# A planned mLSTM + MLP kernel: one pool for the 4 KB tiles, paired Softplus, merged attention products, another planned order

## The chip, the core and the metric

The kernel runs on one core of a Trainium2 chip. The metric is the device time in microseconds (us) of one execution, the median over runs. One more execution was recorded by the hardware profiler; all rows of the trace come from that one.

## The reference, cut to what matters

Four sequences (B) with eight heads (H), 768 steps (S) and head size 40 (D) go through a gated linear attention with a running maximum, and its output, 320 wide, goes token by token through an MLP with Softplus and Erf:

```python
for t in range(S):
    m_new = np.maximum(f_gate[:, :, t] + m, i_gate[:, :, t])
    f_stab = np.exp(f_gate[:, :, t] + m - m_new)
    i_stab = np.exp(i_gate[:, :, t] - m_new)
    C = f_stab * C + i_stab * outer(v_t, k_t);  n = f_stab * n + i_stab * k_t
    y[:, :, t] = sigmoid(o_gate_t) * (C @ q_t) / max(abs(n . q_t), 1)
h = x @ w_in                          # (3072, 320) @ (320, 2048)
g = h * erf(softplus(h))
out = g @ w_out                       # (2048, 320)
```

(shortened; `x` is `y` with the heads side by side). The MLP's weights arrive as 64-bit floats, and all is computed to float32 accuracy.

## The kernel before, in words

**Attention.** Time is cut into six chunks of 128 steps. A chunk of one sequence is an attention step s (24 of them; 0 to 3 are the first chunk). For each chunk a gate part (lines 257 to 322) scans the running maximum, sums the log gates (`scan`, `g`, `sum`, lines 268 to 291) and cuts them into three bf16 pieces (`split`); from the second chunk on twelve small DMAs (`rhs`, line 319) put rows of it into `rhsE`. An attention step (lines 324 to 518) then has these runs on TensorE, each named by its lines:

- pe (367, 369): the exponents of all heads, two PSUM banks, then Exp on ScalarE (375) and the causal mask on POOL (380);
- S (397): the scores, two banks, multiplied into the masked weights on VectorE (412);
- pq (422): the decay of each row, multiplied into q on VectorE (430); only from the second chunk on;
- ph (439, 443): the numerators and denominators from the state and from the chunk itself; pk (455): what the chunk adds to the state, from `vg` (406);
- tr (500): transposes of the step's output (480 to 494), whose high part goes to `xh` (ScalarE, 513) and low part to `xl` (VectorE, 517).

All of these use four PSUM banks, the tag `pa`.

**Weights.** Each of 22 tiles of 512 KB raw weights (12 of `w_in`, 10 of `w_out`) is loaded on SP's queue and decoded from 64-bit words (lines 523 to 548): a first step on ScalarE (530), two bit steps on VectorE (535, 536), a rounded high part on ScalarE (541, tiles `wh`, `woh`) and the low part on POOL (547, `wl`, `wol`). A decode holds one of two work tiles (`bits`) from 530 to 547. The raw tile itself takes a free place among the MLP's own tiles hb, e, gh and gl, of which a few must stay free (`KEEP`).

**MLP.** A block k is 256 tokens, two attention steps. A phase f is half a block's hidden layer (24 phases, the first four in the order (0,0), (1,0), (0,1), (1,1)). A phase has two groups g of 512 hidden units: two up runs of 16 matmuls into the two banks `h` (630), each copied to `hb` (on ScalarE, 639, in the first two phases, then on VectorE, 641), Softplus (648) and Erf (652) on ScalarE, the product with h (VectorE, 656), its rounded part gh (ScalarE, 661) and the rest gl (VectorE, 666), and two down runs of 12 matmuls (691, 692, 694) that add to the banks `po0` and `po1`. High and low parts make each product exact enough: three matmuls in place of one. Exp, Softplus and Erf need three different function tables, and a load of a table (ACT_TABLE_LOAD) stands before each change.

**What sets the order.** Nothing is ordered by hand. `Plan.issue` (lines 77 to 166) holds every part with its engine, cost, table, buffers and targets, lets a list scheduler run in model time, and emits the parts in order of their start; each engine then works in this order, waiting on semaphores. A chain (lines 734 to 748) fixes the order of the table users: both Softplus and then both Erf of a phase, then the Exp of the step that belongs to it (`AHEAD`). `SLOTS` gives the number of buffers of each tag, `FIRST`, `PHASE` and `BEHIND` the targets.

Of the kernel before, what the change touches and what calls it, by code (L numbers as in the profile page):

```python
# [18 lines left out]
L = 128  # L19
# [21 lines left out]
class Buf:  # L41
    def __init__(self, tag=None, keep=None):
        self.tag, self.keep, self.users, self.left = tag, keep, [], 0
# [6 lines left out]
class Plan:  # L50
# [26 lines left out]
    def issue(self):  # L77
# [3 lines left out]
        for p in parts:  # L81
            for x in p.after:
                x.succ.append((p, True))
            for x in p.order:
                x.succ.append((p, False))
            p.wait = len(p.after) + len(p.order)
        topo, left = [p for p in parts if not p.wait], {p.n: p.wait for p in parts}
# [11 lines left out]
        for p in parts:  # L99
            for b in p.held:  # L100
                b.left += 1
        slots = {tag: [0.0] * n for tag, n in self.slots.items()}
# [5 lines left out]
        def can(p):  # L108
            t = max(free[p.engine], p.ready)
            for b in p.new:  # L110
                if b.keep:
                    at = [(min(slots[tag]), i, tag) for i, (tag, n) in enumerate(b.keep.items()) if len(slots[tag]) > n]
                    if not at:
                        return None
                    t, b.tag = max(t, min(at)[0]), min(at)[2]
                    continue
                s = slots[b.tag]
                need = sum(x.tag == b.tag for x in p.new)
                if len(s) < need:
                    return None  # L120
                t = max(t, sorted(s)[need - 1])
            return t + self.TABLE * (p.table is not None and len(p.table) > 1 and table not in p.table)

        while len(out) < len(parts):
# [27 lines left out]
            for b in p.new:  # L152
                slots[b.tag].remove(min(slots[b.tag]))
            for b in p.held:
                b.left -= 1
                if not b.left:
                    slots[b.tag].append(max(u.done for u in b.users if hasattr(u, 'done')))
# [7 lines left out]
        out.sort(key=lambda p: (p.start, out.index(p)) if False else p.start)  # L165
# [3 lines left out]
SLOTS = dict(pa=4, h=2, po0=1, po1=1, qk=3, kvo=3, dm=5, vg=4, xh=2, xl=2, o_sb=4, hb=4, e=3, gh=3, gl=3,  # L169
             bits=2, spl=2, x0=1, gt=1, m_c=2, aL=3, den=2)  # L170
FIRST, PHASE, BEHIND = 20.0, 18.0, 1.3
AHEAD = {s: s - 4 for s in range(B * NC)}
AHEAD.update({0: -1, 1: -1, 2: -1, 3: -1, 4: 2, 5: 2, 6: 3, 7: 3})
KEEP = dict(gl=1, gh=1, e=2, hb=2)
# [4 lines left out]
def tile_mlstm_moe(  # L179
# [23 lines left out]
    def new(pool, shape, dtype, tag):  # L203
        return pool.tile(shape, dtype, name=tag, bufs=SLOTS[tag])

# [51 lines left out]
    def gate_chunk(c):  # L257
# [10 lines left out]
        @make(f'scan{c}', 'DVE', 0.65, after=[load, last.scan if c else p_small], new=[m_c], use=[gt] + ([last.m_buf] if c else []))  # L268
# [8 lines left out]
        @make(f'g{c}', 'DVE', 0.66, after=[scan], new=[x0], use=[gt, m_c])  # L277
        def g():
            v.x0 = new(sb, [128, 3, L], F32, "x0")
            y = v.x0[:, 2]  # L280
            nc.vector.tensor_tensor(y, v.gt[:, 1], v.m[:, 0:L], op=ALU.add)
            nc.vector.tensor_tensor(y, y, v.m[:, 1:L + 1], op=ALU.subtract)
            if c == 0:
                nc.vector.memset(y[:, 0:1], 0.0)

        @make(f'sum{c}', 'DVE', 1.05, after=[g, p_small], use=[gt, m_c, x0])
        def total():
            nc.vector.tensor_tensor_scan(
                out=v.x0[:, 1], data0=v.x0[:, 2], data1=zero.to_broadcast([128, L]), initial=0.0, op0=ALU.add, op1=ALU.add)
            nc.vector.tensor_tensor(v.x0[:, 0], v.gt[:, 0], v.m[:, 1:L + 1], op=ALU.subtract)  # L290
            nc.vector.tensor_tensor(v.x0[:, 0], v.x0[:, 0], v.x0[:, 1], op=ALU.subtract)
# [10 lines left out]
        @make(f'split{c}', 'DVE', 2.6 if c else 1.9, after=[v.exp or total, p_cst], new=[spl], use=[x0])  # L302
# [21 lines left out]
    def attention(s):  # L324
# [16 lines left out]
        def load():  # L341
            t = new(sb, [128, 2, NPR, L], F32, "qk")
# [3 lines left out]
        @make(f'loadv{s}', 'SP', 0.45, kb=484.0, new=[kvb])  # L346
        def loadv():
            n = new(sb, [128, KVO + 64], F32, "kvo")
            nc.sync.dma_start(n[:, 0:KVO], kvo[c, b])
            v.kn = n[:, 0:DM].rearrange("p (h d) -> p h d", d=D)  # L350
            v.v1 = n[:, DM:KV].rearrange("p (h d) -> p h d", d=V1)
            v.th = n[:, KV:KVO]
            v.y = n[:, KV:KVO + 64]

        @make(f'rows{s}', 'POOL', 1.2 if c else 0.5, after=[G.split, p_zeros], use=[G.spl_buf],
# [4 lines left out]
        v.pe, ex, sel = [], [], []  # L360
        for j in range(2):
            @make(f'pe{s}', 'PE', 0.24 if c else 0.46, after=[rowsp, *G.rhs, p_rhsE[c % 2]], new=[peb[j]], target=mid(14 - j),
                  order=[step[s - 2].S] if s > 1 else [])
            def pe(j=j):
                spl = splB[b]
# [4 lines left out]
            v.pe.append(pe)  # L370

            @make(f'ex{s}', 'ACT', 0.5, after=[pe], new=[dmb[j]], use=[peb[j]], table=('exp',))
# [5 lines left out]
            @make(f'sel{s}', 'POOL', 0.85, after=[e], use=[dmb[j]])  # L378
# [6 lines left out]
        @make(f'th{s}', 'ACT', 0.38, after=[loadv], use=[kvb], table=('exp', 'er'))  # L385
        def th():
# [3 lines left out]
        @make(f'S{s}', 'PE', 0.95, after=[load, *ex], new=psb, use=[qkb], mode=1, target=mid(11),  # L390
              order=[step[s - 2].ph_] if s > 1 else [])
        def Sp():
# [427 lines left out]
```

## Time and profile before

| | us |
|---|---|
| median of three runs | 512.39 |
| the runs | 512.39, 510.31, 515.2 |
| the profiled execution | 513.25 |
| its span, first to last instruction | 511.2 |

The profile calls the engines PE (TensorE), PEld (its weight loads), DVE (VectorE), ACT (ScalarE), POOL (GpSimd) and SP (which here only issues DMAs). In a row of a chain or timeline stand the start, the duration and what ran; in a group the line, engine, operation, tiles as out<-in and shapes, the count, the busy time with the mean ns of one, and the idle time before them with what ended it. A matmul's own duration overlaps with its neighbours; in the chain each has only what it adds. "issue" as what ended a wait means that the profile shows nothing that was waited for. The matmuls of the float32 attention products count twice in the trace.

### The profile page before, as it was taken

The page shows a single profiled execution, that of the slowest core. Times are in us where ns is not written, and L with a number is a line of the kernel's source. Part 1 is how long each engine was busy: PE and PEld are TensorE (multiplying, and loading weights), DVE is VectorE, ACT ScalarE, POOL GpSimd, SP SyncE. Part 2 cuts the span into 40 slices and gives each one's busy share as a digit, 9 for nine tenths or more (in the row PEclk, how much of TensorE's full clock was granted, in tenths as well). Part 3 has the DMA queues.
Part 4 walks back from the last instruction along what each step waited for, and adds up shares of the span by engine and source line. Part 5 has one row for each costly group of instructions (what it writes and reads, how often), then busy time and mean ns, then how long its engine had stood idle before and what let it go on. Part 6 is the DMA issues. An engine that isn't in the chain of part 4 may idle for free.

```text
span 511.2 us, 13994 instructions
## 1 busy us (share of the span) xinstructions
PE 470.2 (92%) x6120; PEld 448.2 (88%) x6120; DVE 347.6 (68%) x609; ACT 363.7 (71%) x424; POOL 104.3 (20%) x158
## 2 busy tenths in 40 slices
PE   3497678959999999999999999999999999999977
PEld 2376678949999999999999999999999999999977
DVE  3579859897887766787766885765974665555431
ACT  4268897985357977977977877887787795566651
POOL 5173425272220101121101111001211010000000
PEclk9758797978999999999999999999999999999997
DMA  7999623102261220122131131131131100000000
GB/s 193 281 294 264 168 83 125 55 1 73 64 185 40 73 82 29 66 56 78 54 99 35 42 103 36 40 100 36 40 102 36 39 28 2 3 27 0 27 0 27
DMA packets 17765, 39.40 MB, mean 77 GB/s; under 512 B 2920, under 2 KB 9064, under 8 KB 17704
## 3 DMA queue, kind: packets, MB, share of 16 engines
q1 hardware_dynamic: 17704, 38.51, 26.3%
q8 instruction: 48, 0.79, 0.6%
q14 instruction: 13, 0.11, 0.1%
HBM read 34.45 MB, written 3.93 MB: 75 GB/s over the span
## 4 chain that ended last, share of the span: by engine, by line
PE 78%; DMA 6%; DVE 5%; issue 4%; ACT 4%; POOL 1%; SPq 1%; DVEq 0%; POOLq 0%; ACTq 0%
PE h L630 31%; PE po L691 11%; PE po L692 10%; PE po L694 10%; PE pa L397 4%; DMA kvo<-in_kvo_dram 3%; PE pa L439 3%; PE pa L443 2%; DMA gl<-in_w_in_dram 2%; PE pa L367 2%; PE pa L500 2%; DVE hb L656 1%; PE pa L422 1%; PE pa L455 1%; DVE bits L536 1%
## 5 line engine op out<-in xcount | busy, mean ns | idle before, releaser
L630 PE MATMUL h<-xh,wh 128*128 128x256 f32 x576 | 163.9, 292 | 5.2 <-ACT wh L541 3.4
L630 PE MATMUL h<-xl,wh 128*128 128x256 f32 x576 | 161.7, 288 | 1.2 <-DVE xl L517 0.9
L691 PE MATMUL po<-woh,gh 128*128 128x320 f32 x384 | 124.2, 334 | 3.1 <-ACT gh L661 3.1
L630 PEld LDWEIGHTS h<-xh,wh 128*128 128x128 f32 x576 | 112.4, 195 | 6.7 <-ACT wh L541 3.6
L692 PE MATMUL po<-wol,gh 128*128 128x320 f32 x384 | 116.4, 314 | 0.0
L630 PEld LDWEIGHTS h<-xl,wh 128*128 128x128 f32 x576 | 112.6, 195 | 1.8 <-DVE xl L517 1.2
L630 PE MATMUL h<-xh,wl 128*128 128x256 f32 x384 | 110.8, 289 | 1.4 <-POOL wl L547 1.4
L641 DVE COPY hb<-h 128x512 f32<-128x512 f32 x88 | 60.3, 688 | 67.0 <-PE h L630 66.6
L648 ACT ACT_TABLE_LOAD x40 | 51.3, 1283 | 46.6 <-DVE hb L641 46.2
L656 DVE TENSOR_TENSOR hb<-e,hb 128x1024 f32<-128x1024 f32 x48 | 60.0, 1265 | 32.2 <-ACT e L652 32.1
L691 PEld LDWEIGHTS po<-woh,gh 128*128 128x128 f32 x384 | 73.8, 192 | 6.1 <-ACT gh L661 3.4
L648 ACT ACTIVATE e<-hb 128x1024 f32<-128x1024 f32 x48 | 50.7, 1059 | 39.0 <-DVE hb L641 32.8
L630 PEld LDWEIGHTS h<-xh,wl 128*128 128x128 f32 x384 | 74.8, 195 | 1.7 <-POOL wl L547 1.7
L692 PEld LDWEIGHTS po<-wol,gh 128*128 128x128 f32 x384 | 74.1, 193 | 0.3
L694 PE MATMUL po<-woh,gl 128*128 128x320 f32 x384 | 72.8, 312 | 0.1
L380 POOL TENSOR_SCALAR_AFFINE_SELECT dm<-dm 128x512 f32<-128x512 f32 x48 | 32.6, 698 | 152.0 <-ACT dm L375 151.7
L666 DVE TENSOR_TENSOR gl<-hb,gh 128x1024 fp32r<-128x1024 f32 x48 | 59.5, 1241 | 3.0 <-PE po L694 2.2
L694 PEld LDWEIGHTS po<-woh,gl 128*128 128x128 f32 x384 | 61.2, 191 | 0.4 <-DVE gl L666 0.4
L661 ACT ACTIVATE gh<-hb 128x1024 fp32r<-128x1024 f32 x48 | 50.6, 1057 | 8.3 <-DVE hb L656 7.9
L488 POOL TENSOR_TENSOR kvo<-kvo,den 128x320 f32<-128x320 f32 x24 | 20.1, 836 | 149.7 <-DVE kvo L484 111.1
L652 ACT ACTIVATE e<-e 128x1024 f32<-128x1024 f32 x48 | 48.4, 1051 | 0.3
L412 DVE TENSOR_TENSOR dm<-pa,dm 128x512 f32<-128x512 f32 x48 | 32.0, 684 | 13.2 <-PE pa L397 13.2
(81 smaller groups left out, 614.6 us busy)
## 6 DMA issues: line engine op xcount, KB each, us to landing
kvo<-in_kvo_dram SPq DMA_DIRECT2D x24, 484.0 KB
qk<-in_qk_dram SPq DMA_DIRECT2D x24, 416.0 KB
out_dram<-o_sb SPq DMA_DIRECT2D x24, 160.0 KB
gh<-in_w_in_dram SPq DMA_DIRECT2D x3, 512.0 KB
gl<-in_w_in_dram SPq DMA_DIRECT2D x4, 256.0 KB
gl<-in_w_in_dram SPq DMA_DIRECT2D x2, 512.0 KB
e<-in_w_in_dram SPq DMA_DIRECT2D x2, 512.0 KB
hb<-in_w_out_dram SPq DMA_DIRECT2D x3, 320.0 KB
```

Of the source, the lines that this page charges most:

```text
L380: nc.gpsimd.affine_select(out=v.w[j], in_=v.w[j], pattern=[[0, NPR], [1, L]], compare_op=ALU.is_ge, fill=0.0, base=0, channel_multiplier=-1)
L412: nc.vector.tensor_tensor(v.w[j], v.ps[j], v.w[j], op=ALU.mult)
L630: nc.tensor.matmul(V.h[i][:, n % 2 * T:(n % 2 + 1) * T], w, m, start=(q == 0), stop=(q == len(ops) - 1))
L641: nc.vector.tensor_copy(V.hb[:, i * 512:(i + 1) * 512], V.h[i])
L648: nc.scalar.activation(V.e, V.hb, AF.Softplus)
L652: nc.scalar.activation(V.e, V.e, AF.Erf)
L656: nc.vector.tensor_tensor(V.hb, V.e, V.hb, op=ALU.mult)
L661: nc.scalar.activation(V.gh, V.hb, AF.Copy)
L666: nc.vector.tensor_tensor(V.gl, V.hb, V.gh.bitcast(F32), op=ALU.subtract)
L691: nc.tensor.matmul(K.po[b], V.gh[:, ts], woh[:, w], start=start, stop=False)
L692: nc.tensor.matmul(K.po[b], V.gh[:, ts], wol[:, w], start=False, stop=False)
L694: nc.tensor.matmul(K.po[b], V.gl[:, ts], woh[:, w], start=False, stop=stop)
```

## The change

- **One pool.** The tags qk, kvo, hb, e, gh and gl (3 + 3 + 4 + 3 + 3 + 3 places) become one tag `big` with 19 places of 4 KB. Raw weights are tiles of it too; `CAPS` limits each kind in the planner (raw: 10), and `KEEP` holds back places. To fit into 4 KB, K, V and the output gate of a step come by two DMAs, and y lies over the gate and k.
- **Paired Softplus.** For the phases in `BURST` (0, 2, 4, 6 to 20) the first Softplus also waits for the copies of the second group.
- **Merged runs.** The two halves of pe are one part, pq is at the head of S, pk at the tail of ph, and steps follow each other more strictly (S of a step after ph of the step before).
- **Moved work.** The gate steps `g` and the new `rest` go from VectorE to POOL; `vg` of steps 1, 2, 3, 5 and 7 too; copies of h for phases 0 to 4 and 6 (not 0 and 1) are on ScalarE; six low parts (`LO_DVE`) go from POOL to VectorE; the state copy of step 1 goes to ScalarE.
- **The order.** Costs in the planner are altered, the penalty for a change of table is doubled, and `NUDGE`, a table of some 190 numbers, shifts the due times of single parts.

```diff
-SLOTS = dict(pa=4, h=2, po0=1, po1=1, qk=3, kvo=3, dm=5, vg=4, xh=2, xl=2, o_sb=4, hb=4, e=3, gh=3, gl=3,
+SLOTS = dict(pa=4, h=2, po0=1, po1=1, big=19, dm=5, vg=4, xh=2, xl=2, o_sb=4,
              bits=2, spl=2, x0=1, gt=1, m_c=2, aL=3, den=2)
...
+CAPS = dict(qk=4, kvo=4, hb=4, e=3, gh=3, gl=3, raw=10)
...
+KEEP = {'raw': 4, 'qk': 1, 'kvo': 1}
+HB_ACT = {0, 1, 2, 3, 4, 6}
+BURST = {0, 2, 4, 6, 7, 8, 9, 10, 11, 12, 13, 14, 15, 16, 17, 18, 19, 20}
+LO_DVE = {'i01', 'i30', 'i31', 'o0', 'o2', 'o6'}
+GATE = {1: 0, 2: 3, 3: 7, 4: 11, 5: 15}
+VG_POOL = {1, 2, 3, 5, 7}
+SK_ACT = {1}
+NUDGE = {
+    'S0': 15.8, 'S1': 0.2, 'S2': 13.8, 'S4': 4.2, 'S5': -3.1, 'S6': 1.5, 'S7': -7.1, 'deci10': -17.8,
...
+    def big(name, dtype=F32, n=1024):
+        return sb.tile([128, n], dtype, name=name, tag="big", bufs=SLOTS["big"], padded_shape=[128, 1024])
...
-            n = new(sb, [128, KVO + 64], F32, "kvo")
-            nc.sync.dma_start(n[:, 0:KVO], kvo[c, b])
...
+            n = big("kvo")
+            nc.sync.dma_start(n[:, DM:KVO], kvo[c, b][:, 0:KV])
+            nc.sync.dma_start(n[:, 0:DM], kvo[c, b][:, KV:KVO])
...
         def Sp():
+            if c > 0:
+                v.pq_ = t = bank(NPR, L)
+                for p in range(NPR):
+                    nc.tensor.matmul(t[:, p], selP[:, 2 * p:2 * p + 2].rearrange("p a b -> p (a b)"),
+                                     splB[b][:, 1, :], start=True, stop=True)
             v.ps = [bank(NPR, L) for _ in range(2)]
...
+    for f, v in enumerate(phases):
+        if f in BURST:
+            v.sp[0].after.extend(v.copies[2:])
```

The counts of matmuls are the same in both programs; table loads are 100 before and 70 now. Three places of the two orders follow, each before and then now.

ScalarE, from the Softplus of phase 2 to the first Exp of step 4 (e is the tile of Softplus, or of Erf where it is also the input; bits, wh and woh are decode; dm the exponents; hb the copies of h):

```order
L648 ACT_TABLE_LOAD
L648 ACTIVATE e<-hb 128x1024
L541 ACTIVATE woh<-bits 128x512
L530 ACT_TABLE_LOAD
L530 ACTIVATE bits<-gh 128x512
L530 ACTIVATE bits<-e 128x512
L648 ACT_TABLE_LOAD
L648 ACTIVATE e<-hb 128x1024
L652 ACT_TABLE_LOAD
L652 ACTIVATE e<-e 128x1024 x2
L375 ACT_TABLE_LOAD
L375 ACTIVATE dm<-pa 128x512
```

```order
L684 ACTIVATE hb<-h 128x512
L694 ACT_TABLE_LOAD
L694 ACTIVATE e<-hb 128x1024 x2
L698 ACT_TABLE_LOAD
L698 ACTIVATE e<-e 128x1024 x2
L422 ACT_TABLE_LOAD
L422 ACTIVATE dm<-pa 128x512 x2
```

The two Softplus stand in a row behind the last copy, the decode steps are ahead of them, and five table loads became three.

SP's queue, the last loads of the output weights (raw now; gl, hb and e before) and the twelve small rows of the second chunk's gates (rhsE):

```order
L594 DMA gl<-in_w_out_dram 128x256
L594 DMA hb<-in_w_out_dram 128x640
L594 DMA hb<-in_w_out_dram 128x384
L594 DMA e<-in_w_out_dram 128x512 x2
L319 DMA rhsE_69<-spl 1x8x128 x6
L594 DMA hb<-in_w_out_dram 128x384
L594 DMA hb<-in_w_out_dram 128x640
L319 DMA rhsE_69<-spl 1x8x128 x6
```

```order
L620 DMA raw<-in_w_in_dram 64x1024 x2
L363 DMA rhsE_69<-spl 1x8x128 x3
L607 DMA raw<-in_w_in_dram 128x1024 x2
L363 DMA rhsE_69<-spl 1x8x128 x9
L639 DMA raw<-in_w_out_dram 128x384
L639 DMA raw<-in_w_out_dram 128x640
L307 DMA gt<-in_gates_dram 128x2x128
L639 DMA raw<-in_w_out_dram 128x128
```

The gate rows now go ahead of the last five tiles of the output weights, where they stood behind four of them.

TensorE at the end (of every down run only its last row, four matmuls with gl, is shown; gl's number tells the group, po0 and po1 the two halves of the tokens), from the last matmul of the last up run on:

```order
L630 MATMUL h_6559<-xl_5965,wh_79 128x256
L694 MATMUL po0_6531<-woh_81,gl_6527 128x320 x4
L694 MATMUL po1_6546<-woh_81,gl_6527 128x320 x4
L694 MATMUL po0_6531<-woh_81,gl_6609 128x320 x4
L694 MATMUL po1_6546<-woh_81,gl_6609 128x320 x4
L694 MATMUL po0_6531<-woh_81,gl_6613 128x320 x4
L694 MATMUL po1_6546<-woh_81,gl_6613 128x320 x4
```

```order
L675 MATMUL h_6539<-xl_6003,wh_79 128x256
L740 MATMUL po1_6343<-woh_81,gl_6416 128x320 x4
L740 MATMUL po0_6574<-woh_81,gl_6499 128x320 x4
L740 MATMUL po0_6574<-woh_81,gl_6521 128x320 x4
L740 MATMUL po1_6605<-woh_81,gl_6499 128x320 x4
L740 MATMUL po1_6605<-woh_81,gl_6521 128x320 x4
L740 MATMUL po0_6574<-woh_81,gl_6621 128x320 x4
L740 MATMUL po1_6605<-woh_81,gl_6621 128x320 x4
L740 MATMUL po0_6574<-woh_81,gl_6637 128x320 x4
L740 MATMUL po1_6605<-woh_81,gl_6637 128x320 x4
```

The last phase's four down runs are the last four in both; ahead of them stand two before and five now.

More of the change, by code (lines that the diff above doesn't have):

```diff
@@ L275, in gate_chunk @@
         v.scan = scan
-        @make(f'g{c}', 'DVE', 0.66, after=[scan], new=[x0], use=[gt, m_c])
+        @make(f'g{c}', 'POOL', 1.0, after=[scan], new=[x0], use=[gt, m_c])
         def g():
@@ L300, in gate_chunk @@
         n = 3 if c > 0 else 2
[L302 removed]
+        @make(f'split{c}', 'DVE', 3.0 if c else 2.0, after=[v.exp or total, rest, p_cst], new=[spl], use=[x0])
         def split():
@@ L358, in rowsp, with pe @@
             nc.gpsimd.tensor_copy(splB[b][rows], G.spl[rows, 0:(3 if c > 0 else 2):(2 if c > 0 else 1)])
[L360 to L365, printed above, removed]
+        ex, sel = [], []
+        @make(f'pe{s}', 'PE', 0.42 if c else 0.86, after=[rowsp, *G.rhs, p_rhsE[c % 2]], new=peb, target=mid(14), mode=3,
+              order=[step[s - 1].S] if s > 0 else [])
+        def pe():
+            spl = splB[b]
+            for j in range(2):
                 v.pe_[j] = t = bank(NPR, L)
@@ L369, in pe @@
                     nc.tensor.matmul(t[:, p], r[:, 2 * p + j, :], spl[:, 1, :], start=False, stop=(p == NPR - 1))
-            v.pe.append(pe)
-            @make(f'ex{s}', 'ACT', 0.5, after=[pe], new=[dmb[j]], use=[peb[j]], table=('exp',))
+        v.pe = [pe]
+        for j in range(2):
+            @make(f'ex{s}', 'ACT', 0.56, after=[pe], new=[dmb[j]], use=[peb[j]], table=('exp',))
             def e(j=j):
@@ L413, in attention @@
             w.append(wp)
-        v.pq, qa = None, None
+        v.pq, qa = Sp, None
         if c > 0:
-            @make(f'pq{s}', 'PE', 0.26, after=[rowsp, p_selP], new=[pqb], target=mid(9),
-                  order=[step[s - 1].ph_, Sp])
-            def pq():
-                v.pq_ = t = bank(NPR, L)
-                for p in range(NPR):
-                    nc.tensor.matmul(t[:, p], selP[:, 2 * p:2 * p + 2].rearrange("p a b -> p (a b)"),
-                                     splB[b][:, 1, :], start=True, stop=True)
-            v.pq = pq
-            @make(f'qa{s}', 'DVE', 0.83, after=[pq, load], new=[aLb], use=[pqb, qkb], order=[Sp])
+            @make(f'qa{s}', 'DVE', 0.83, after=[Sp, load], new=[aLb], use=[pqb, qkb])
             def qa():
@@ L444, in ph @@
                                          start=(c == 0), stop=(c == 0 or j == 1))
+            if not last:
+                v.pk = bank(NPR, V1)
+            for p in range(0 if last else NPR):
+                for d in (slice(0, 32), slice(32, D)):
+                    for j in range(2):
+                        nc.tensor.matmul(v.pk[64 * j + d.start:64 * j + d.stop, p], v.kn[:, 2 * p + j, d], v.vg[j][:, p],
+                                         start=True, stop=True)
         v.ph_ = ph
@@ L521, in tile_mlstm_moe, with decode @@
     wout = []
-    def decode(name, raw, rawb, ready, hi, lo, engine='POOL'):
+    def decode(name, raw, rawb, ready, hi, lo):
+        engine = 'DVE' if name in LO_DVE else 'POOL'
         v = SimpleNamespace()
         vb = Buf('bits')
-        @make(f'val{name}', 'ACT', 0.58, after=ready, new=[vb], use=[rawb], table=('exp', 'er'))
+        @make(f'val{name}', 'ACT', 0.7, after=ready, new=[vb], use=[rawb], table=('exp', 'er'))
         def val():
```

163 lines of the change are left out of this document (83 added, 80 removed), and 22 rows, old and new, of the table NUDGE.

## The prediction

> **What bounds the kernel now.** I read the page first, then the busy time by stage, the chain that ended last, TensorE's waits, and ScalarE's groups in the stage where TensorE has holes. The page's first line:
>
> ```profile
> PE 470.2 (92%) x6120; PEld 448.2 (88%) x6120; DVE 347.6 (68%) x609; ACT 363.7 (71%) x424; POOL 104.3 (20%) x158
> ```
>
> 92% is an average over stages that have different limits. Busy time by stage, the cuts set where TensorE's behaviour changes:
>
> ```profile
> 0.00:39.90 39.90, 23.16 (x420) 18.71 (x422) 23.09 (x51) 18.69 (x31) 19.25 (x37) 0.79 0.94 260
> 39.90:110.80 70.90, 54.80 (x461) 51.02 (x459) 60.42 (x93) 60.99 (x84) 32.26 (x28) 0.86 0.43 117
> 110.80:115.80 5.00, 3.59 (x130) 3.00 (x130) 4.12 (x8) 4.94 (x6) 1.77 (x2) 0.50 0.01 3
> 115.80:491.30 375.50, 375.22 (x5048) 362.56 (x5045) 254.57 (x455) 271.79 (x298) 50.99 (x92) 1.00 0.18 54
> 491.30:511.20 19.90, 13.42 (x72) 12.89 (x70) 5.43 (x5) 7.33 (x8) 0.00 (x0) 0.81 0.05 17
> ```
>
> After the stretch and its length come busy us of PE, PEld, DVE, ACT, POOL, then granted clock, DMA share, GB/s. From 115.8 to 491.3 TensorE has 0.28 us free at clock 1.00. Nothing can be won there without fewer matmuls, and the matmul counts of the two programs are equal. ScalarE has 104 us free in it. What can be won lies before 115.8 us (first the loads at 0.94 of the DMA engines, then ScalarE at 61.0 of 70.9 us and VectorE at 60.4) and in the last 20 us. The end of the chain:
>
> ```profile
> 467.29 3.83 PE h L630 x32
> ...
> 489.32 1.93 PE h L630 x16
> 491.27 0.70 DVE hb L641
> 492.05 1.06 ACT e L648
> 493.13 1.28 ACT L652
> 494.43 1.07 ACT e L652
> 495.52 1.24 DVE hb L656
> 496.77 1.07 ACT gh L661
> 497.88 0.64 PE po L691
> ...
> 501.45 0.27 PE po L691
> ...
> 504.32 0.15 PE po L691
> ...
> 507.89 0.44 ACT o_sb L712
> ```
>
> and two of TensorE's waits (total, times, longest):
>
> ```profile
> PE pa L443 <- issue: 6.4, 1, 6.4
> ...
> PE po L691 <- ACT gh L661: 3.1, 1, 3.1
> ```
>
> The last up run ends at 491.25. Its results pass copy, Softplus, table load, Erf, product and rounding, and are there at 497.84, 6.6 us later. Only two down runs stand in between, so TensorE is idle for 3.1 us, and the next two runs go at a slow clock: 497.88 to 501.45 is 3.57 us and 501.45 to 504.32 is 2.87 us, where the last two, at the full clock, take 1.78 each (504.32 to 507.89).
>
> **The change part by part.**
>
> *The tail.* In the new order nine down runs, not six, follow the last up run: five instead of two lie ahead of the first that needs its results. Five by 1.78 is 8.9 us against the 6.6 us chain, so the wait goes (3.1 us) and with it the slow clock (3.57 + 2.87 - 2 x 1.78 = 2.9). One output copy now stands between the two Erf on ScalarE (0.44 by L712); it holds only the second half, which is needed two runs later. **-6.0 us**; bounds -3.1 (the clock stays slow) and -6.4.
>
> *The stage where ScalarE and VectorE are the limit.* Eight down runs and sixteen up runs precede the first down run of phase 2 in both programs. Before, it starts at 115.79, after the last weight has been decoded:
>
> ```profile
> 39.93 1.28 ACT L648 ACT_TABLE_LOAD   x1
> ...
> 110.17 0.63 ACT L541 ACTIVATE woh<-bits 128x512 fp32r<-128x512 f32 x1 [0.66 <-DVE bits L536]
> ```
>
> ```profile
> 109.56 3.01 POOL L547 TENSOR_TENSOR wol<-bits,woh 128x512 fp32r<-128x512 f32 x2
> ```
>
> ```profile
> 115.79 0.64 PE L691 MATMUL po<-woh,gh 128*128 128x320 f32 x1
> ```
>
> ScalarE's groups between these two points, 39.9 to 110.8 us:
>
> ```profile
> L648 ACT ACT_TABLE_LOAD x5 | 6.4, 1283 | 0.1
> L648 ACT ACTIVATE e<-hb 128x1024 f32<-128x1024 f32 x6 | 6.3, 1057 | 0.1
> ...
> L541 ACT ACTIVATE woh<-bits 128x512 fp32r<-128x512 f32 x10 | 6.0, 623 | 1.6 <-DVE bits L536 1.6
> ...
> L652 ACT ACT_TABLE_LOAD x3 | 3.8, 1283 | 0.0
> L639 ACT ACTIVATE hb<-h 128x512 f32<-128x512 f32 x6 | 3.6, 592 | 3.2 <-PE h L630 3.2
> L530 ACT ACTIVATE bits<-gl 128x512 f32<-128x512 f32 x5 | 3.4, 673 | 0.7 <-POOL wol L547 0.7
> ...
> L530 ACT ACT_TABLE_LOAD x2 | 2.6, 1283 | 0.0
> ...
> L297 ACT ACT_TABLE_LOAD x1 | 1.3, 1283 | 0.0
> L375 ACT ACT_TABLE_LOAD x1 | 1.3, 1283 | 0.0
> L513 ACT ACTIVATE xh<-pa 128x384 fp32r<-128x384 f32 x2 | 1.0, 481 | 0.0
> ```
>
> That is 12 table loads. Between the same two points the new order has 9. It has one Softplus more, two first decode steps and three high-part copies fewer (they come earlier, when ScalarE is half idle), two transposed copies fewer and four copies of h more (moved from VectorE): -3 x 1.283 + 1.057 - 2 x 0.673 - 3 x 0.623 - 2 x 0.481 + 4 x 0.592 = -4.6 us of work. Of the 9.9 us idle I let half go, 4.9: VectorE, whose decode it waits for, gives copies of h and gate steps away, and loads no longer wait for one of few buffers; bounds 0 and 9.9. The first Softplus I leave at 40: it now waits for all four copies of phase 0, but the input weights are loaded ahead of the later attention tiles. It could start 6.4 us earlier if TensorE's pause of 6.4 us inside an attention product (all its inputs there) does not come back. So the last high part ends at 40 + 70.9 - 4.6 - 4.9 = 101.4, its low part needs 1.5 more on POOL (half of 3.01), and products of step 4 and scores of step 5 go first: I take 4.0 in all, where it took 5.0. First down run of phase 2 at 105.4, **-10.4 us**; bounds -4 and -17. The new order has also done the scores of step 5 by then (1.1 us by L397's row below): **-1.1**. Steps 4 and 5 follow each other closely, and the score run of step 4 has only one exponent run behind it to cover VectorE: **+1.5**; 0 to 5.
>
> By the Trainium skill, ScalarE: Activation LUTs, "What ACT_TABLE_LOAD costs", a switch costs 1.28 us and a drain of 1.38 more; the estimate from that page for three loads is -8.0 in place of -3.8. The trace does not show the drain: above, a Softplus ends at 493.11, the load starts at 493.13 and the Erf at 494.43.
>
> *All the other table loads* (27 of the 30 that go) lie after 115.8, where TensorE hides ScalarE: nothing. What pays for them is that the first Softplus of a phase waits for the fourth copy. Before, one phase in the steady stage reads
>
> ```profile
> 240.22 1.28 ACT L648 ACT_TABLE_LOAD   x1 [3.20 <-DVE hb L641]
> ...
> 250.46 1.09 ACT L375 ACTIVATE dm<-pa 128x512 f32<-128x512 f32 x2
> ```
>
> ```profile
> 252.98 1.16 PE L397 MATMUL pa<-qk 40*128 40x128 f32 x16
> ```
>
> The exponents end at 251.55, the score run that reuses their banks starts at 252.98: 1.4 us of cover. Now one more Softplus (about 1.0) lies in that queue, and the row-decay products (some 0.2 us) go ahead of the scores: 0.7 us of cover are left. I cost it at nothing; if it is gone, see the third rival.
>
> *Merged products:* in the steady stage both orders have the same four attention runs for a step, and over all 292 runs stand for 300. A boundary costs little (two up runs in one piece take 3.83 us, two apart 2 x 1.93): 0, at most -0.3. *The shared pool:* raw tiles get places of their own; its worth is in the idle time above. *K/V/O in two pieces:* 24 more DMA issues on SP's queue at
>
> ```profile
> 43.34 0.33 SPq L349 DMA_DIRECT2D kvo<-in_kvo_dram  x1
> ```
>
> one each: 2.6 us over the eight of the first stage, 0.1 us for each piece of weight behind them; hidden, because those loads are bound by bytes. *Gate steps and some vg on POOL, six low parts on VectorE:* POOL's low part takes 1.30 us for 512 columns; before 115.8 six less are -7.8, and eight vg of 164 and twelve gate steps of 128 columns at that rate +7.2. Nothing, but a collision is dear:
>
> ```profile
> 61.29 2.33 DVE L656 TENSOR_TENSOR hb<-e,hb 128x1024 f32<-128x1024 f32 x1
> ```
>
> ```profile
> 61.23 1.30 POOL L547 TENSOR_TENSOR wol<-bits,woh 128x512 fp32r<-128x512 f32 x1 [3.07 <-ACT woh L541]
> ```
>
> 2.33 beside a POOL instruction, 1.24 alone.
>
> **Sum.** The profiled execution: 513.25, its span 511.2. 511.2 - 6.0 - 10.4 - 1.1 + 1.5 = 495.2, and 2.05 around it give 497.25. The median of the three runs, 512.39, is 0.86 below the profiled time: **496.4 us**.
>
> **The rivals.**
>
> 1. *The first stage tightens fully.* The pause of 6.4 us doesn't return, Softplus starts at 36 and all idle time of ScalarE goes: another -4 and -5.0, 487 us. For it: raw tiles are no longer held back, and DMA is busy for 0.43 of the stretch only. Against: VectorE has 60.4 us of work in the same 70.9, so both queues would have to be nearly gapless.
>
> 2. *Only the tail is won.* The decode stays as slow, because its two work tiles, not ScalarE, set its pace: a decode holds one of them from its first step on ScalarE to its low part on POOL, and there are two in both programs. Then phase 2's first down run stays at 115.8: 496.4 + 10.4 = 507 us. For it: ScalarE waits for decode steps of VectorE (1.6) and for POOL's low parts (0.7) in the groups above. Against: 3.2 of its idle time, the largest piece, belong to copies that wait for TensorE.
>
> 3. *Slower: the exponents come late for the scores.* In the steady stage the last copy of a phase queues behind two VectorE instructions of 1.24 each. Everything on ScalarE shifts by 2.5 us, 1.8 more than its cover, and TensorE waits in each of sixteen steps: +28, 525 us. It decides from 0.7 + 16.0/16 = 1.7 us of delay on (there it eats the gain). For it: the fourth copy was the last of two short queues and is now ahead of all. Against: VectorE is busy for 254.6 of 375.5 us, and 72 copies against 88 remain on it.
>
> That the program doesn't do what it says is no rival: the table loads (100 to 70) and the tail stand in its order.
>
> **How the numbers follow.** Forecast 0.59, first rival 0.17, second 0.15, third 0.09. The forecast's own range, from the bounds of its terms, is 489 to 505. The whole range, **485 to 510**, takes in the first rival but for its far end, and the second; about 0.2 is left out. A measurement of this kernel tells about 1%, 5.1 us, from no change. Faster by more: 0.59 + 0.17 + 0.06 of the second (it lies on the bound) = 0.82. Within 1%: 0.09 of the second and 0.02 of the third, 0.11. Slower: 0.07.
>
> **What would show it.** The tail is right if TensorE has no wait of over 0.3 us after its last up run and clock 1.00 to the end. The first stage is right if the first down run of phase 2 starts at 101 to 110 us and ScalarE's stretch before the last high part has 9 table loads. The cover is right if in the steady stage TensorE waits for no bank of the exponents; a wait there of over 1 us for each step makes the prediction wrong, as does a first down run of phase 2 at 115 or later. Loads at over 250 GB/s past 51 us would say that bytes, not engines, set the first stage.

## The result and the profile after

The changed kernel takes 496.23 us, the median of four runs (496.03 to 496.45); the kernel before, run beside it, 513.37 (510.31 to 515.2). The ratio is 0.967, with a 95% interval of 0.962 to 0.972. The forecast was 496.4. The profiled execution is one of the four: 496.05, its span 494.3. The page's first line, and the busy time by stage with the cuts at the first Softplus table load, the end of the last decoded weight, and the steady stage:

```profile
PE 464.1 (94%) x6120; PEld 442.2 (89%) x6120; DVE 327.4 (66%) x562; ACT 333.6 (67%) x412; POOL 113.4 (23%) x187
```

```profile
0.00:42.40 42.40, 26.98 (x564) 22.26 (x564) 29.24 (x63) 24.30 (x44) 29.70 (x55) 1.00 0.96 261
42.40:103.00 60.60, 49.39 (x446) 45.98 (x446) 45.70 (x66) 56.31 (x78) 25.25 (x27) 0.89 0.55 155
103.00:110.00 7.00, 6.82 (x65) 6.25 (x69) 6.45 (x11) 5.30 (x9) 2.22 (x2) 0.52 0.25 77
110.00:478.00 368.00, 367.91 (x4971) 354.96 (x4963) 241.23 (x421) 242.05 (x278) 56.23 (x104) 1.00 0.17 49
478.00:494.30 16.30, 12.99 (x89) 12.73 (x87) 4.80 (x4) 5.61 (x8) 0.00 (x0) 1.00 0.09 31
```

The second row answers to the stretch of 70.9 us before: it is 60.6 now, with ScalarE busy for 56.31 and VectorE for 45.70 (60.99 and 60.42 before). The fourth shows a TensorE without a hole at clock 1.00, as before. The last has no slow clock any more. The three points on which the forecast hung, from ScalarE's and TensorE's timelines:

```profile
42.38 1.28 ACT L694 ACT_TABLE_LOAD   x1
...
102.39 0.61 ACT L586 ACTIVATE woh<-bits 128x512 fp32r<-128x512 f32 x1
```

```profile
94.15 1.16 PE L449 MATMUL pa<-qk 40*128 40x128 f32 x14 [1.44 <-ACT dm L422]
...
97.60 0.59 PE L413 MATMUL pa<-rhsE,splB 128*128 128x512 bf16 x1 [1.97 <-DVE qk L473]
...
103.18 2.05 PE L449 MATMUL pa<-qk 40*128 40x128 f32 x14 [0.57 <-DVE kvo L528]
105.16 0.63 PE L737 MATMUL po<-woh,gh 128*128 128x320 f32 x1
```

The first Softplus table load comes at 42.38 (39.93 before), the last high part ends at 103.0 (110.80), and the first down run of phase 2 starts at 105.16 (115.79). The chain that ended last, from the last up run on:

```profile
473.23 1.92 PE h L675 x16
475.15 0.15 PE po L737
...
490.41 0.60 PE po L740 x4
491.03 0.44 ACT o_sb L758
```

From 475.15 to 491.01 nine down runs follow without a wait, 1.76 us each.

Three lengths cut each execution at two places that all programs have, the first Softplus table load and the first down run of phase 2: the time to the one, the **stretch** from the one to the other, and the **rest** to the end. Before: 39.93, 75.86, 395.41. After: 42.38, 62.78, 389.14. The experiments are read by these, since the length ahead of the first cut varies between programs for a reason of its own (the last experiment but one). Each is read from one profile: among programs that leave the stage between the two cuts alone (after, t_undo, s_unpair, s_delay, a_warm) the stretch goes from 61.33 to 63.40, so a difference of 1 us in it is not clear.

| kernel | median us | ratio to before, 95% | first Softplus | stretch | rest |
|---|---|---|---|---|---|
| before, again (b_again) | 512.03, one run | | 40.99 | 75.81 | 393.20 |
| before, tail alone (t_alone) | 507.88, of three | 0.986 to 0.991 | | | |
| before, extra products (b_warm) | 514.23 | 0.997 to 1.003 | 40.77 | 75.97 | 394.06 |
| after | 496.23 | 0.962 to 0.972 | 42.38 | 62.78 | 389.14 |
| after, tail undone (t_undo) | 505.43 | 0.979 to 0.987 | 45.48 | 61.87 | 395.85 |
| after, steady pairs undone (s_unpair) | 497.41 | 0.966 to 0.971 | 45.65 | 62.79 | 388.96 |
| after, exponents delayed (s_delay) | 510.40 | 0.990 to 0.995 | 45.19 | 63.40 | 401.31 |
| after, early pairs undone (f_unpair) | 504.78 | 0.979 to 0.988 | 42.32 | 69.80 | 389.08 |
| after, gl twice (f_gl2) | 503.49 | 0.975 to 0.984 | 42.66 | 68.56 | 389.28 |
| after, low parts twice (f_lo2) | 503.86 | 0.978 to 0.985 | 44.15 | 69.43 | 388.62 |
| after, low parts back on POOL (u_lo) | 500.36 | 0.969 to 0.977 | 44.05 | 62.95 | 390.50 |
| after, extra products at the start (a_warm) | 498.48 | 0.967 to 0.976 | 45.20 | 61.33 | 389.17 |
| after, waits filled (w_fill) | 496.08 | 0.961 to 0.969 | 42.44 | 61.66 | 389.80 |

The profiled execution of t_alone was disturbed (2326 us), so its trace is not read and only its other three times count: 507.38, 507.88, 508.02.

### The profile page after: what moved, and what is told of

It reads as the page before. It is cut to its first block, busy times and chain, and to the rows that moved or that the text cites. A ratio compares the mean times of both kernels' runs of the same rounds, so it can differ in the third digit from the quotient of the medians.

```text
span 494.3 us, 14040 instructions
## 1 busy us (share of the span) xinstructions
PE 464.1 (94%) x6120; PEld 442.2 (89%) x6120; DVE 327.4 (66%) x562; ACT 333.6 (67%) x412; POOL 113.4 (23%) x187
## 4 chain that ended last, share of the span: by engine, by line
PE 78%; DVE 7%; DMA 6%; ACT 5%; issue 2%; SPq 1%; POOL 0%; ACTq 0%; DVEq 0%
PE h L675 31%; PE po L737 12%; PE po L740 11%; PE po L738 11%; PE pa L449 4%; PE pa L482 3%; PE pa L486 2%; DMA raw<-in_w_out_dram 2%; DMA qk<-in_qk_dram 2%; DVE bits L580 2%; DVE bits L581 2%; PE pa L413 2%; PE pa L544 1%; DMA raw<-in_w_in_dram 1%; PE pa L493 1%
## 5 line engine op out<-in xcount | busy, mean ns | idle before, releaser
L675 PE MATMUL h<-xl,wh 128*128 128x256 f32 x576 | 159.7, 285 | 1.3 <-DVE xl L561 1.3
L737 PE MATMUL po<-woh,gh 128*128 128x320 f32 x384 | 119.7, 323 | 0.9 <-ACT woh L586 0.9
L738 PE MATMUL po<-wol,gh 128*128 128x320 f32 x384 | 114.8, 311 | 1.2 <-POOL wol L592 1.2
L686 DVE COPY hb<-h 128x512 f32<-128x512 f32 x72 | 49.6, 689 | 65.5 <-PE h L675 65.4
L738 PEld LDWEIGHTS po<-wol,gh 128*128 128x128 f32 x384 | 72.9, 190 | 1.5 <-POOL wol L592 1.4
L702 DVE TENSOR_TENSOR hb<-e,hb 128x1024 f32<-128x1024 f32 x48 | 57.6, 1225 | 21.3 <-ACT e L698 20.7
L427 POOL TENSOR_SCALAR_AFFINE_SELECT dm<-dm 128x512 f32<-128x512 f32 x48 | 30.8, 663 | 139.3 <-ACT dm L422 139.1
L532 POOL TENSOR_TENSOR kvo<-kvo,den 128x320 f32<-128x320 f32 x24 | 21.7, 906 | 128.9 <-DVE kvo L528 128.8
L464 DVE TENSOR_TENSOR dm<-pa,dm 128x512 f32<-128x512 f32 x48 | 30.9, 683 | 5.1 <-PE pa L449 4.1
```

Source lines behind the costliest of these rows:

```text
L427: nc.gpsimd.affine_select(out=v.w[j], in_=v.w[j], pattern=[[0, NPR], [1, L]], compare_op=ALU.is_ge, fill=0.0, base=0, channel_multiplier=-1)
L464: nc.vector.tensor_tensor(v.w[j], v.ps[j], v.w[j], op=ALU.mult)
L675: nc.tensor.matmul(V.h[i][:, n % 2 * T:(n % 2 + 1) * T], w, m, start=(q == 0), stop=(q == len(ops) - 1))
L686: nc.vector.tensor_copy(V.hb[:, i * 512:(i + 1) * 512], V.h[i])
L702: nc.vector.tensor_tensor(V.hb, V.e, V.hb, op=ALU.mult)
L737: nc.tensor.matmul(K.po[b], V.gh[:, ts], woh[:, w], start=start, stop=False)
```

## The experiments

The edits keep the planned order and change the list of parts behind `parts = plan.issue()`. `move(name, i, to, j)` puts the i-th part of a name directly ahead of the j-th of another.

### The tail

t_alone gives the kernel before the new tail alone:

```diff
     parts = plan.issue()
+    move('up23', 3, 'dn22', 0)
```

> The kernel before with one edit: its last up run goes ahead of the first two down runs of phase 22, so four instead of two down runs cover the 6.6 us chain. Theory: 4 x 1.78 = 7.1 us cover 6.6, the wait of 3.1 and the slow clock of 2.9 go, 512.4 - 6.0 = 506.4 us. Rival (only the wait goes): 509.3 us. Second rival (the copy of the last up run now queues behind other work of VectorE and the chain gets longer than 7.1): 1 to 3 us less gain, with the wait still to be seen.

Measured: 513.81 (the kernel before, seven runs beside it) - 507.88 = 5.9 us less, 4.8 to 7.2 by the interval. The theory's 6.0 holds, 3.1 for the wait alone does not. That the wait itself is gone can be seen in the trace of after only.

t_undo takes the tail out of the changed kernel:

```diff
     parts = plan.issue()
+    for name, i in (('dn21', 3), ('dn22', 0), ('dn22', 1)):
+        move(name, i, 'up23', 3)
```

> The changed kernel with three down runs put back ahead of the last up run, so that two instead of five of them cover the chain copy, Softplus, table load, Erf, product, rounding. Theory (tail worth 6.0): TensorE waits 3.1 us for the rounded copy after two runs, the next two runs go at the slow clock (about 3.6 and 2.9 us instead of 1.78), the time is 496.2 + 6.0 = 502.2 us. Rival (the slow clock does not hang on this wait): only the 3.1 us come back, 499.3 us. No effect beyond noise would say that the tail of the changed kernel is not what made it end sooner.

Measured: the rest is 395.85 instead of 389.14, +6.7. The median, 505.43, is 3.2 above the 502.2 expected: of the 9.2 between it and after's, the profile shows another 2.2 ahead of the rest (first down run of phase 2 at 107.35). And it was not the wait that I had expected. Chain and TensorE's largest waits:

```profile
480.65 1.93 PE h L675 x16
482.60 0.70 DVE hb L686
...
485.69 1.06 ACT e L698
486.75 0.33 ACT o_sb L758
487.12 0.63 PE po L737
...
491.49 0.15 PE po L738
```

```profile
PE po L737 <- ACT o_sb L758: 4.6, 1, 4.6
```

The two down runs that I had left for cover write the second accumulator, whose last contents are copied out by an instruction that stands behind the first Erf in ScalarE's queue. So they cover nothing: TensorE waits for 4.6 us at once, and then runs at half clock until 491.49, which costs the other 2.1. In the changed kernel that same copy is hidden, because three down runs that do not need it go first. So this run gives the price of a tail without cover, but not the tail of the kernel before. Cover has to be counted in runs that are free to start, not in runs that stand there.

### The steady stage

s_unpair takes the pairing of Softplus back in phases 7 to 20:

```diff
     parts = plan.issue()
+    for f in range(7, 21):
+        move(f'sp{f}', 1, f'er{f}', 1)
```

> The changed kernel with the second Softplus of phases 7 to 20 put back directly ahead of its own Erf, so each of these phases loads two tables more (28 loads, 28 x 1.283 = 35.9 us of ScalarE between 110 and 478 us). Theory (TensorE hides ScalarE there): 496.2 us, within 1 us, no new wait of TensorE. Rival (fewer table loads are what made the steady stage hold): the exponents come later by a load or two, 1.3 to 2.6 us, and with a cover of 0.7 us TensorE loses 0.6 to 1.9 us in each of 14 phases, 505 to 523 us.

Measured: the rest is 388.96, 0.2 less than after. The row of the steady stage:

```profile
110.00:478.00 368.00, 368.00 (x4984) 354.80 (x4984) 243.60 (x425) 279.07 (x306) 56.43 (x104) 1.00 0.17 49
```

ScalarE works 37 us more (279.07 against 242.05), and TensorE has no hole. The 28 table loads are worth nothing here. (The median is 1.2 above after's; in the profile the first Softplus comes 3.3 later.)

s_delay lengthens the exponents of the same stage:

```diff
-                nc.scalar.activation(dm, v.pe_[j], AF.Exp)
+                for _ in range(5 if j == 0 and s >= 8 else 1):
+                    nc.scalar.activation(dm, v.pe_[j], AF.Exp)
```

> The changed kernel with the first exponent of each step from the ninth on computed five times, so that the exponents of 16 steps end 4 x 0.49 = 2.0 us later. The prediction took 0.7 us of cover behind them: TensorE would wait 1.3 us in each step, +21 us, 517 us. The changed kernel's trace shows a cover of 1.35 to 1.7 us: it would wait 0.3 to 0.65 us, +5 to +10 us, 501 to 507 us. If the cover is over 2 us, or the order gives way, nothing changes: 496.5 us.

Measured: the rest is 401.31, +12.2, or 0.76 us for each of 16 steps. The delay was larger than written: an exponent stretch of one step of s_delay and of after,

```profile
307.65 3.60 ACT L423 ACTIVATE dm<-pa 128x512 f32<-128x512 f32 x6
```

```profile
314.68 1.08 ACT L422 ACTIVATE dm<-pa 128x512 f32<-128x512 f32 x2
```

differ by 2.52 us. So the cover is 2.52 - 0.76 = 1.8 us, not the 0.7 of the prediction, by which 29 us would have gone. The waits stand only in part in the list of waits; I read the rest of them from the score runs' groups, s_delay's from 112 to 488 us and after's from 108 to 484, as longer busy time, 6.3 us beside 2.6 idle. That is 8.9 of the 12.2 us; another 2.5 are single waits of other runs (1.44 for an output copy, 0.76 and 0.30). By the score runs alone the cover would be 2.0:

```profile
L450 PE MATMUL pa<-qk 40*128 40x128 f32 x288 | 27.2, 289 | 2.6 <-ACT dm L423 2.3
```

```profile
L449 PE MATMUL pa<-qk 40*128 40x128 f32 x288 | 20.9, 285 | 0.0
```

The median, 510.40, lies above the 501 to 507 expected from a cover of 1.35 to 1.7, because the delay was 2.5 us and not 2.0, and because the first Softplus came 2.8 later.

### The stage before 105 us: three doses

Each of three kernels adds some 7 to 10 us of work to one engine between the first Softplus and the last decoded weight.

ScalarE, by six table loads:

```diff
     parts = plan.issue()
+    for f in (0, 1, 2):
+        move(f'sp{f}', 1, f'er{f}', 1)
```

> The changed kernel with the second Softplus of phases 0, 1 and 2 put back directly ahead of its own Erf: six table loads more between the first Softplus and the last decoded weight, 6 x 1.283 = 7.7 us of ScalarE. Theory (ScalarE's own time sets this stage, with 4.3 us idle in 60.6): the stretch from the first Softplus table load to the first down run of phase 2, 62.8 us, grows by 5 to 7.7 us, 501 to 504 us. Rival (the decode's two work tiles, or VectorE, set its pace): it grows by less than 2 us, 496 to 498 us.

GpSimd, by eight low parts done twice, which also holds their work tiles longer:

```diff
+TWICE = {'o1', 'o3', 'o5', 'o7', 'o8', 'o9', 'i20', 'i21'}
...
-            e.tensor_tensor((lo or hi)()[h], v.val[h], hi().bitcast(F32)[h], op=ALU.subtract)
+            for _ in range(1 + (name in TWICE)):
+                e.tensor_tensor((lo or hi)()[h], v.val[h], hi().bitcast(F32)[h], op=ALU.subtract)
```

> The changed kernel with eight of the low parts on GpSimd computed twice, so eight decodes hold their work tile 1.3 us longer, 10.4 us in all, on an engine that is busy for 25 of the 60.6 us. Theory (ScalarE sets the stage): the stretch from the first Softplus table load to the first down run of phase 2 grows by 0 to 2.5 us (the last low part itself is 1.3), 496 to 499 us. Rival (the two work tiles set the pace): each longer hold delays the next decode, +5 to +10 us, 501 to 506 us.

VectorE, by six rounding remainders done twice:

```diff
-                nc.vector.tensor_tensor(V.gl, V.hb, V.gh.bitcast(F32), op=ALU.subtract)
+                for _ in range(1 + (f < 3)):
+                    nc.vector.tensor_tensor(V.gl, V.hb, V.gh.bitcast(F32), op=ALU.subtract)
```

> The changed kernel with the rounding remainders of phases 0, 1 and 2 computed twice on VectorE: six more instructions of some 1.2 us, 7.2 us, between the first Softplus and the last decoded weight, on an engine that is busy for 45.7 of the 60.6 us. ScalarE's six table loads gave +7.0 and GpSimd's eight longer low parts +6.65 in the stretch from the first Softplus table load to the first down run of phase 2 (62.8 us). Theory (the decode is one chain that passes ScalarE, VectorE and GpSimd with two work tiles, so time on any of the three shows): +4 to +7 us, 500 to 504 us. Rival (only ScalarE and the hold of the tiles count, VectorE has 15 us free): 0 to +2 us, 496 to 499 us.

Measured, as growth of the stretch: ScalarE +7.0 for a dose of 7.7, VectorE +5.8 for 7.2, GpSimd with the tiles +6.7 for 10.4. The theory that ScalarE alone sets this stage falls: f_lo2 was expected at 0 to 2.5 and came out where its rival stood. ScalarE's waits for a low part, in f_lo2 and in after:

```profile
ACT bits L576 <- POOL wol L594: 5.0, 4, 1.7
```

```profile
ACT bits L575 <- POOL wol L592: 0.2, 1, 0.2
```

In after the two work tiles are free just in time; held 1.3 us longer they stop ScalarE four times. The dose on VectorE comes back in the same way: ScalarE waits 7.1 us for VectorE's bit steps in f_gl2, and 1.8 in after.

```profile
ACT woh L586 <- DVE bits L581: 4.1, 4, 1.5
ACT wh L586 <- DVE bits L581: 3.0, 2, 2.2
```

And the last wait of TensorE ahead of the first down run is for VectorE in each program, though not for a decode: L528 belongs to the output of attention step 4, which stands in VectorE's queue with the decode. It is 0.57 us in after (the row at 103.18), and in f_gl2

```profile
109.24 2.04 PE L449 MATMUL pa<-qk 40*128 40x128 f32 x14 [1.98 <-DVE kvo L528]
```

So a decode, with the attention steps in the same queues, is one chain through three engines with little slack between them, and a microsecond of these doses was worth 0.6 to 0.9 us of the stretch. The medians of f_unpair and f_gl2 (504.78 and 503.49) lie 1.9 and 1.3 us above their profiled executions, so the stretches are the lower reading of these two.

u_lo takes back the move of six low parts to VectorE:

```diff
-            e = nc.vector if engine == 'DVE' else nc.gpsimd
+            e = nc.gpsimd
```

> The changed kernel with one part undone: the six low parts that it moved to VectorE are on GpSimd again (1.30 instead of 0.69 us each). Two of them lie ahead of the first Softplus, four behind it. From the doubled low parts (+6.65 us for 8 x 1.3): 4 x 0.6 = 2.4 us of longer hold give +1 to +2.5 us, and VectorE next to a busy GpSimd gets slower; 497 to 500 us. Rival (VectorE is the tighter of the two, so the move cost as much as it gave): within 1 us, 496 to 497 us.

Measured: the stretch grows by 0.2 only, but the first down run of phase 2 then stops inside, waiting for its low part:

```profile
108.98 0.64 PE L738 MATMUL po<-wol,gh 128*128 128x320 f32 x1 [0.81 <-POOL wol L592]
```

and the rest is 1.4 longer. Together 1.5, within the 1 to 2.5 expected; but the same sum is 451.92 in after, 451.75 in s_unpair and 450.50 in a_warm, so 1.5 is hardly more than what separates programs without this edit. The other 1.7 of its longer span lie ahead of the first Softplus (44.05), where a pause of TensorE that after does not show took 1.1, so that the 4.1 between the medians are not the price of this move alone.

### TensorE's pause of 6.4 us

b_again is the kernel before, unedited:

> The kernel before once more, unedited, for a second profile of it. If the 6.4 us pause of TensorE inside an attention product without a wait belongs to the program, it is there again at the same instruction, with a granted clock near 0.79 in the first 40 us. If it was an accident of one execution, it is elsewhere or gone, and the first up run and the first Softplus come sooner; the time then says whether the later stage absorbs it (513 either way) or not (507).

Measured: TensorE pauses for 6.93 us at the same matmul. The clock of the first 40 us is 0.79 again, and the rest is 2.2 us shorter, of which more at the end.

```profile
PE pa L443 <- issue: 6.9, 1, 6.9
```

The pause belongs to the program. Another, of 4.82 us at L455, is something else: it stands in both profiles of this kernel after 877 pairs, with the DMA engines idle, and in b_warm (next), 120 pairs later, at the same instruction. Each time it ends 0.10 us after VectorE's L430, which reads the bank of the row decay. The kernel before:

```profile
112.21 0.76 PE L455 MATMUL pa<-vg,kvo 128*32 128x41 f32 x32 [4.82 <-issue]
```

```profile
111.44 0.67 DVE L430 TENSOR_TENSOR qk<-qk,pa 104x512 f32<-104x512 f32 x1
```

So I take it for a wait for that bank: L430 stood behind two decodes in VectorE's queue. It is the largest wait of TensorE in this stage, close ahead of the first down run of phase 2, and in after the wait for the same operation is 1.97 us (the row at 97.60, L473 there).

Back to the first pause. Pairs that TensorE had executed when it stopped and, 6.3 us later, when it had not yet gone on, in the kernel before:

```profile
0.00:16.90 16.90, 8.08 (x221) 6.21 (x222) 8.38 (x25) 8.31 (x12) 7.24 (x24) 1.00 0.85 216
0.00:23.20 23.20, 8.08 (x221) 6.21 (x222) 9.99 (x27) 8.31 (x12) 8.66 (x26) 0.91 0.89 221
```

s_unpair stops after 222 pairs too, at a different instruction (L493, 1.4 us):

```profile
0.00:24.60 24.60, 10.64 (x222) 8.02 (x222) 13.34 (x31) 11.73 (x19) 14.57 (x37) 1.00 0.93 231
```

So the place seems to go with a number of instructions, not with an operand. b_warm and a_warm move the count:

```diff
     parts = plan.issue()
+    def warm():
+        t = new(ps, [128, 512], F32, 'po0')
+        for i in range(60):
+            nc.tensor.matmul(t[0:32, 0:41], ident[:, i % 2 * 32:i % 2 * 32 + 32], ident[:, 0:41], start=True, stop=True)
...
+    parts.insert(at('ident') + 1, w)
```

> The kernel before with 60 small extra products of the identity matrix (their result is not used) as TensorE's first instructions, 120 of its load-and-multiply pairs. In four profiles TensorE pauses without a wait after exactly 221 or 222 pairs, whatever instruction stands there, and resumes some 3 us after a 16 KB packet of the instruction queue has landed (between 20 and 22 us). Theory (TensorE waits for its own instructions, whose packet stands behind data): the same count is now reached about 100 pairs into the work, the packet is asked for at 4 to 5 us, when the queues are short, and lands before it is needed; the pause of 6.4 to 6.9 us at the attention product goes or is below 2, the first up run starts at 29 to 30 us instead of 32.3 to 33.3, the first Softplus 2 to 3 us sooner, and the time is 2 to 3 us less, about 511. Rival (the pause belongs to that product and its operands): it stays at the same product, 513.5 us. Second rival: the pause goes, but weights that land late set the first Softplus, 513 us.

> The changed kernel with the same 60 extra products at the start. Two of its three profiles so far had a pause of 1.4 us after 222 pairs and the first down run of phase 2 at 107.4 to 108.4 us, one had none and 105.2. Theory (instructions): no pause after that count, first down run of phase 2 at 105 us in each execution, 495.5 to 497 us. Rival (the pause hangs on the attention products): 1.4 us in most executions, 496 to 499 us.

Measured: the pause did not go, and the time is the same (514.23 against 513.88). But it moved. TensorE now stops for 0.17 us only at 222 pairs (15.37) and pauses 7.2 us at the next boundary, 128 pairs on:

```profile
24.13 0.50 PE L443 MATMUL pa<-kvo,dm 128*32 128x41 f32 x15 [7.23 <-issue]
```

```profile
0.00:24.10 24.10, 12.47 (x349) 11.32 (x350) 10.53 (x27) 7.95 (x12) 8.17 (x26) 0.93 0.90 228
```

In a_warm it is at 349 pairs as well (1.4 us; the time, 498.48, is not the 495.5 to 497 expected). The extra products are 120 pairs, so in the program itself the pause moved by only 7 or 8 pairs; but both times it stands in the middle of a run, behind 49 of 64 matmuls in b_warm (41 before) and behind 7 of 32 in a_warm (ahead of the run in s_unpair). 128 pairs are 256 instructions, and in every profile with such a pause one 16 KB packet of the instruction queue lands 2.4 to 3.1 us ahead of the end of the pause (48 of them carry 0.79 MB over the span); in the kernel before within 20.25 to 20.5 us, for the go at 23.24. The row of that queue, the kernel before from 20.0 to 20.5:

```profile
q8 instruction: 1, 0.02, 16.8%
```

What fits all of this is that TensorE waits for its own instructions. The rival (operands of that product) would have kept the pause where it was in the program. My theory's second half, that an earlier request ends the pause, is wrong: the next packet comes as late, while the DMA engines are at 0.9 and small attention products use up 128 pairs in 1.8 us (15.0 to 16.8 in b_warm). That the packet is late because it stands behind data was not tried by itself. In after the packet lands at 19.4 to 19.5, and pair 222 is reached at some 22.6 only, because TensorE was waiting for exponents (1.71 us): the pause is gone by a coincidence of less than 1 us. Its relatives, nearly the same program up to there, run without a pause (f_unpair, f_gl2, w_fill: first Softplus at 42.3 to 42.7) or with one of 0.9 to 1.4 us (t_undo, s_unpair, s_delay, f_lo2, u_lo: 44.0 to 45.7).

By the Trainium skill, Runtime: NRT & Kernel Launch, "Instruction fetch mechanics", instructions come in 16 KiB blocks of 256. The step of 128 pairs agrees. It also says that the fetch is hidden behind the issue rate; the pauses of 6.4 to 7.2 us here disagree.

### The waits at steps 4 and 5

w_fill puts extra products into TensorE's three waits there:

```diff
+    def fill(n):
+        for _ in range(n):
+            nc.tensor.matmul(block[1].pot[:, 320:448], selP[:, 0:2].rearrange("p a b -> p (a b)"),
+                             splB[0][:, 1, :], start=True, stop=True)
...
+                fill(20 * (s == 5 and j == 1))
...
+                    fill({4: 15, 5: 5}.get(s, 0) * (p == 0 and j == 1))
```

> The changed kernel with small extra products (their result is not used) in TensorE's three waits at steps 4 and 5, 15, 20 and 5 of them, sized below the waits of 1.44, 1.97 and 0.57 us. In the changed kernel TensorE's granted clock is 0.5 from the second wait at 97.6 to 109.8 us. Theory (the waits, not the work, cost the clock): the clock stays at or near 1.0 there, the first down run of phase 2 starts 1 to 1.5 us sooner and the runs behind it are not slow (2.2 us), 3 to 3.6 us less in the stretch from the first Softplus table load to step 110, 492.5 to 494 us. Rival (ScalarE and VectorE set this stretch and the clock is hidden behind them): within 1 us of 496.2. Second rival (the extra products are in the way): up to 2 us slower.

Measured: the same time (496.08 against 496.23). From 100 to 102 us, after and then w_fill:

```profile
100.00:102.00 2.00, 2.00 (x77) 1.70 (x70) 1.97 (x3) 1.97 (x3) 2.00 (x3) 0.50 0.22 38
```

```profile
100.00:102.00 2.00, 2.00 (x116) 1.72 (x105) 1.97 (x4) 1.99 (x2) 2.00 (x3) 1.00 0.18 29
```

The clock was kept, TensorE got through the attention products in less time, and then waited longer: 0.71 us instead of 0.57 at the same score run, on top of the 0.45 that were filled, and 1.69 for an exponent that had not been waited for at all. The first down run came 1.1 us sooner, stopped inside for VectorE's low part (0.41 us), the clock fell at 105 us, and 0.7 were given back. So the rival holds: the waits, not the work, cost the clock, but the other engines set the pace. A slow clock costs little where TensorE waits for others anyway.

## Why the prediction was right

| term | predicted | measured |
|---|---|---|
| tail | -6.0 | -5.9 (t_alone) |
| first Softplus | 40.0, no change | 42.38, +2.4 |
| ScalarE's work to the last high part | -4.6 | -4.7 (60.99 to 56.31) |
| ScalarE's idle time there | -4.9 | -5.6 (9.9 to 4.3) |
| last high part to first down run | 5.0 to 4.0 | 5.0 to 2.2 |
| first down run of phase 2 | 105.4 | 105.16 |
| scores of step 5 | -1.1 | about -0.3 (rest -6.27, less the tail's -6.0) |
| waits at steps 4 and 5 | +1.5 | -1.6 (5.6 to 4.0), within the front |
| steady stage | 0 | 0 |

- **The total** is nearer than its terms. The span was forecast as 495.2 and is 494.3; the 0.86 that the forecast took off because the profiled execution before lay above its median does not show after (496.05 against 496.23). The two nearly cancel, which is luck.
- **The tail** is right in size and cause. Its part for the clock is not certain in every execution: in b_again the same wait of 3.1 us left the clock at 1.00 (below).
- **The front** is right in its sum by errors that cancel, which is luck too. The step that failed is "the first Softplus I leave at 40". Two copies of h stand ahead of it in ScalarE's order before, and four now, with two more transposed copies and the decode steps that the prediction itself moved there (two first steps, three high parts). It comes 2.4 us later, though the first up run starts 2.8 sooner (29.48); that this work is the reason was not tried by itself. The last leg, taken at 4.0, was 2.2. The work and the idle time of ScalarE in between are as worked out, to 0.7 us.
- **"ScalarE and VectorE are the limit"** was right as a heading, but the second rival was put too sharply against it: its work tiles are one more limit beside ScalarE, not instead of it. That the tiles did not stop the gain is because the change also shortened the chain elsewhere: six low parts went to VectorE (some 1.5 us, by u_lo, hardly clear), and VectorE lost 14.7 us of work in the stretch. Letting half of the idle time go was a choice without a mechanism. The doses supply one, since time taken from VectorE shows too. What the shared pool gave to it was not tried, and neither was the planner without `NUDGE`.
- **The cover in the steady stage** was mis-sized (0.7; it is 1.8 to 2.0), at no cost to the forecast. The third rival would have needed a delay of more than that to show at all. Its premise is wrong too: in this stage, where VectorE makes the copies, the first Softplus of a phase does not wait for the fourth. `BURST` binds the planner alone, and gives the kernel no wait; only the second Softplus waits, for its own copies:

```profile
299.58 1.06 ACT L694 ACTIVATE e<-hb 128x1024 f32<-128x1024 f32 x1
304.48 1.06 ACT L694 ACTIVATE e<-hb 128x1024 f32<-128x1024 f32 x1 [3.84 <-DVE hb L686]
```

- **The waits at steps 4 and 5** are 4.0 us in the trace (1.44, 1.97 and 0.57), in the range of 0 to 5. But they are not an addition: the kernel before waits 5.6 us at the same place, 0.80 and the 4.82 at L455, which the prediction did not count. They lie ahead of the first down run, where VectorE and ScalarE would have held TensorE up anyway: filled, they are worth 0.4 us of span.
- **The first rival** needed the pause to vanish and Softplus to start at 36. The pause did vanish in after, and Softplus still came at 42.38, so the pause alone does not set it. It does seem to matter: in the relatives of after with a pause of 0.9 to 1.4 us the first Softplus comes 1.7 to 3.3 us later.

## What to carry to other kernels

Where three engines pass one tile on, price the chain and not its busiest engine: a dose of dummy work on each engine in turn tells which of them has slack, and busy shares do not (VectorE had 15 of 60.6 us free and still passed on 0.8 of each microsecond). Read what ended just before a wait that the profile puts down to "issue": one of the two here was another engine's queue. Count cover in runs whose own operands and accumulators are free at that moment. And where a stage is hidden behind a full engine, savings in it, 36 us of table loads here, are worth nothing until they leave the stage.

## What the runs showed of the hardware

- The instruction queue brings 16 KB packets by DMA, and TensorE can run out of instructions; the runs fit this, none tried the packet by itself. While the loads keep the DMA engines at 0.9, a block of 128 load-and-multiply pairs of small products (1.8 us) can end before the next has come: pauses of 0.2 to 7.2 us without a wait, at about 222 or 350 pairs, and once (0.66) at 476.
- A wait does not fix what follows it in the clock. The same 3.1 us of the same program were followed by a slow clock in one execution and by none in another. Before, then b_again, each behind the wait of its tail:

```profile
500.00:505.00 5.00, 5.00 (x24) 5.00 (x23) 0.29 (x1) 0.00 (x0) 0.00 (x0) 0.62 0.00 0
```

```profile
500.00:505.00 5.00, 5.00 (x36) 4.92 (x34) 1.64 (x2) 0.47 (x2) 0.00 (x0) 1.00 0.01 3
```

The rest of b_again is 2.2 us shorter (393.20 against 395.41). In after, waits of 1.44 and 1.97 us (the rows at 94.15 and 97.60) were followed by 12 us at about 0.50. The Trainium skill, TensorE: Matmul & The Clock Gate, "HAM oscillation — how this bites in real kernels", gives gaps of over some 3.4 us as the rule; the two shorter waits here disagree with it as a threshold for one gap. Its section "What's actually happening" says that the window is free-running, so that the moment of the change varies from run to run; b_again agrees with that.
